# Attention followed by a mixing block on one core: local attention's result turned in 64x64 tiles for two chunks at once, the transposed x kept in staging tiles, and a new order

## The chip, the cores and the metric

The kernel runs on one core of one Trainium2 chip. The core has a matrix engine (TensorE, "PE" in the profile, with its weight loads as "PEld"), a vector engine (VectorE, "DVE"), an activation engine (ScalarE, "ACT"), a general one (GpSimd, "POOL") and one that only issues transfers (SyncE, "SP"). Matmuls write PSUM, eight banks of 512 float32 columns on 128 partitions; all else lies in SBUF. The metric is the time of one execution on the device, in microseconds (us); the figure given for a kernel is the median of its runs.

## The reference

Two parts follow each other. The first is an attention with a coarse and a local branch, for 8 batches, 8 heads, 576 positions and 64 values a head:

```python
q_d = q.reshape(B, H, Sd, factor, D).mean(axis=3)      # factor 4, so 144 positions; k_d, v_d alike
out_d = sm_attn(q_d, k_d, v_d)
out_up = np.repeat(out_d, factor, axis=2)
mask = np.abs(pos[:, None] - pos[None, :]) < factor
scores = scale * np.matmul(q, k.transpose(0, 1, 3, 2))
scores = np.where(mask, scores, -1000000000.0)
...
out_local = np.matmul(attn, v)
return (out_up + out_local).astype(np.float32)
```

Its result, 576 rows of 512 a batch, is the x of the second:

```python
theta = x @ w_theta
zr, zi = x * np.cos(theta), x * np.sin(theta)
y = np.einsum('ts,bsd->btd', w_tok_r, zr) + np.einsum('ts,bsd->btd', w_tok_i, zi)
u = x + y
return (u + np.maximum(u @ w_ch, 0.0)).astype(np.float32)
```

## The kernel before

All matmuls are in bfloat16. The work of a batch is cut into steps, and each step is a small function that issues a few instructions on one engine. `ORDER` is one long list of two-letter words, each with a place behind it (a PSUM bank or two, a staging tile, or the engine that does a copy: v, a or g for DVE, ACT, POOL). The program goes through the list and ties each instruction to the one before it on its engine, so every engine runs its instructions strictly in the order of the list; among engines only data and buffers make them wait. SP issues the loads, the stores and the transposing transfers, in that same order. Nothing else schedules; how the list came about is not in the program.

A batch goes like this. q and k are loaded in float32 into staging tiles (`lq`, `lk`, 14 tiles of 576 columns), cast (`cq`, `ck`), transposed on PE (`tp`, nine 128x128 blocks a step) and copied out of PSUM (`ev`); for the last batch transfers do the turning. Means over four positions (`kd`, `qd`), the coarse scores (`sd`), their exponentials on ACT (`ed`), the coarse result (`nd`), its division (`xn`) and turn (`xd`, `xc`) give xdT, the coarse part with channels on partitions.

The local branch cuts the 576 positions into ten windows of 64 (58 of them own rows), two windows to a chunk, so five chunks. `ps` makes scores for two chunks at once (32 matmuls in 64x64 tiles, L483), `ex` their exponentials, `mk` the multiplication with the band, `po` the product with v of one chunk (16 matmuls in 64x64 tiles, L512), `nm` divides by the row sums (L520 and L521) into tmp. In tmp 64 rows of a window stand twice, heads 0 to 3 on the first 64 partitions and 4 to 7 on the others. `xt` (L524 to L533) turns it: four matmuls of the whole array a chunk, tmp as weights and 116 columns of the identity, into one bank. `xa` (L535 to L541, DVE) adds xdT, each column four times, and writes xT, which is x with channels on partitions.

From xT `th` makes theta (L548, four matmuls of 512 columns for 128 rows), `cs` cosine and sine on ACT. x is also wanted with rows on partitions: `xm` turns it on PE, and for batches 6 and 7 (`XDMA`) `dx` does so with four transposing transfers on SP into one buffer xx (L589). `zz` (L592) multiplies it with cosine and sine. The last 64 rows of a batch take a way of their own (`tt`, `ct`, `zt`, `zp` or `dz`, `zc`). `mx` multiplies with the token weights, nine matmuls of 288 columns a step (L610), `ua` adds x (L615), `ch` is the product with w_ch (L635), `up`/`uc` or `du` turn u back, `rl` (L638, DVE) takes the maximum and adds, `st` stores 128 rows. `ht`, `rt`, `ss`, `sr` do the same for the last 64 rows of two batches at once.

`wm` puts matmuls of zeros into the list where PE would stand still; they compute nothing. 46 of them and six ahead of the list stand in the first 20 us. `te` and `ts` have ACT load the table of exponentials or of sines.

## Time and profile before

| What | Figure |
|---|---|
| Median of three runs | 235.89 us (235.51 to 235.91) |
| The profiled execution | 236.41 us |
| Its span, first to last instruction | 234.7 us |
| PE busy | 223.5 us, 95% of the span |
| DVE, ACT, POOL busy | 187.6, 159.7, 143.9 us |
| Mean granted clock of PE | 0.997 of full speed |
| Transfers | 49.35 MB, 210 GB/s on the mean |

The span lies within the execution; 1.7 us are outside it. In the views of the trace a row of time reads: start in us, length in us, engine, line, operation, tile written and tiles read, shape, number of such instructions in a row, and in brackets how long the engine had been idle and what ended that. A row of groups reads: line, engine, operation, tiles, shape and count, then busy time and the mean of one in ns, then idle time ahead of them. 128\*128 or 64\*64 ahead of a matmul's shape is the part of the array in use, rows by columns. The length of a matmul has its way through the array in it, so two in a row overlap; how long PE is taken by one is the difference between its start and that of the next. "issue" is time in which an engine waited for nothing that the profile shows. A stretch reads: from, to, its length, the busy time and count of PE, PEld, DVE, ACT and POOL, the granted clock, the busy share of the transfer engines, and GB/s.

### The profile page before, as it was taken

To read this page: it belongs to the slowest core of one execution; us is meant where nothing else is said; L and a number is where in the kernel's file an instruction comes from. 1 tells how busy PE (TensorE), PEld (TensorE's weight loads), DVE (VectorE), ACT (ScalarE), POOL (GpSimd) and SP (SyncE) were. 2 spreads that over 40 slices of the span, in tenths; PEclk is the share of its full clock that TensorE was granted. 3 is DMA by queue.
4 is the path that set the end of the run, shared out by engine and by line. 5 is a ranking of instruction groups with operands and counts; after the bars stand their busy time and mean duration, and the time that the engine had idled before them with its cause. 6 is when DMAs were issued, how large, how long until landed. Compare 5 with 4: busy or idle time off the path is not lost.

```text
span 234.7 us, 8524 instructions
## 1 busy us (share of the span) xinstructions
PE 223.5 (95%) x3500; PEld 155.7 (66%) x3500; DVE 187.6 (80%) x377; ACT 159.7 (68%) x239; POOL 143.9 (61%) x190
## 2 busy tenths in 40 slices
PE   7998899999999699999999999899999999999992
PEld 3555767687787466786688757676676665577740
DVE  5169997999898689888799869969898879466472
ACT  2389898669987779869987796859889358510000
POOL 7858999809999995983874628794598310100000
PEclk9999999999999999999999999999999999999998
DMA  6999979996959999999986206996967357674477
GB/s 196 383 392 386 287 163 276 391 244 143 290 162 250 243 345 212 224 224 244 287 183 173 61 0 141 292 236 139 127 155 169 73 124 197 91 221 109 110 226 244
DMA packets 76647, 49.35 MB, mean 210 GB/s; under 512 B 61120, under 2 KB 61120, under 8 KB 76608
## 3 DMA queue, kind: packets, MB, share of 16 engines
q1 hardware_dynamic: 76608, 48.81, 81.4%
q8 instruction: 27, 0.44, 0.8%
q14 instruction: 12, 0.10, 0.2%
HBM read 33.98 MB, written 9.44 MB: 185 GB/s over the span
## 4 chain that ended last, share of the span: by engine, by line
PE 85%; DVE 8%; issue 3%; DMA 2%; ACT 1%; SPq 0%; DVEq 0%
PE PS L610 29%; PE PS L635 12%; PE PS L548 10%; PE PS L304 5%; PE PS L531 3%; PE PS L512 3%; PE PS L715 3%; PE PS L587 2%; PE PS L483 2%; DMA z<-zT 2%; PE PS L275 2%; DVE tmp L521 2%; PE PS L448 2%; PE PS L624 2%; PE PS L652 1%
## 5 line engine op out<-in xcount | busy, mean ns | idle before, releaser
L610 PE MATMUL PS<-WT,z 128*128 128x288 bf16 x576 | 77.9, 286 | 0.4 <-DMA z<-zT 0.4
L610 PEld LDWEIGHTS <-z 128*128 128x128 bf16 x576 | 54.3, 98 | 16.0 <-DMA z<-zT 0.7
L615 DVE TENSOR_TENSOR uT<-PS,xT 128x288 bf16<-128x288 f32 x64 | 28.8, 452 | 12.4 <-PE PS L610 11.9
L548 PE MATMUL PS<-wth,xT 128*128 128x512 bf16 x128 | 32.2, 379 | 0.0
L635 PE MATMUL PS<-wch,uT 128*128 128x512 bf16 x128 | 31.1, 379 | 0.0
L569 POOL TENSOR_TENSOR zT<-xT,cst 128x512 bf16<-128x512 bf16 x7 | 8.1, 1153 | 35.9 <-ACT cst L566 27.6
L521 DVE TENSOR_TENSOR tmp<-PS,rl 128x512 bf16<-128x512 f32 x40 | 27.6, 691 | 1.4
L502 POOL TENSOR_TENSOR pm<-pm,band 128x1024 bf16<-128x1024 bf16 (+1 forms) x14 | 25.1, 1792 | 5.5 <-ACT pm L491 5.5
L537 DVE TENSOR_TENSOR xT<-PS,xdT 128x464 bf16<-128x464 f32 (+1 forms) x40 | 24.0, 628 | 4.5 <-PE PS L531 2.3
L640 DVE SCALAR_TENSOR_TENSOR osb<-PS,ur 128x512 f32<-128x512 f32 x32 | 21.8, 684 | 5.2 <-PE PS L635 4.9
L491 ACT ACTIVATE pm<-PS 128x1024 bf16<-128x1024 f32 (+1 forms) x24 | 20.4, 880 | 6.4 <-PE PS L483 6.4
L553 ACT ACTIVATE cs<-PS,pihc 128x512 bf16<-128x512 f32 x32 | 22.1, 692 | 3.0 <-PE PS L548 2.8
L331 POOL TENSOR_TENSOR two<-kT 128x580 f32<-128x580 bf16 x13 | 15.0, 1154 | 9.4 <-ACT kT L317 6.6
L720 ACT ACT_TABLE_LOAD x15 | 19.2, 1283 | 0.3
L635 PEld LDWEIGHTS <-uT 128*128 128x128 bf16 x128 | 11.9, 98 | 11.1
L554 ACT ACTIVATE cs<-PS 128x512 bf16<-128x512 f32 x32 | 19.2, 600 | 0.0
L594 DVE TENSOR_TENSOR z<-PS,cs 128x1024 bf16<-128x1024 bf16 x24 | 16.0, 681 | 2.4 <-PE PS L587 2.1
L548 PEld LDWEIGHTS <-xT 128*128 128x128 bf16 x128 | 11.2, 98 | 9.8 <-DVE xT L537 0.4
L438 ACT ACTIVATE pd<-PS 128x864 bf16<-128x864 f32 x16 | 13.8, 888 | 5.6 <-PE PS L427 5.6
L331 POOL TENSOR_TENSOR two<-qT 128x576 f32<-128x576 bf16 x13 | 14.9, 1148 | 4.3 <-ACT qT L317 4.0
L397 POOL CAST v_w<-st 128x512 bf16<-128x512 f32 x26 | 16.2, 647 | 0.0
L531 PE MATMUL PS<-ident,tmp 128*128 128x116 bf16 (+1 forms) x160 | 13.9, 215 | 2.1 <-issue 2.0
(116 smaller groups left out, 435.8 us busy)
## 6 DMA issues: line engine op xcount, KB each, us to landing
st<-in_k_dram SPq DMA_DIRECT2D x32, 288.0 KB, 5.3
st<-in_q_dram SPq DMA_DIRECT2D x32, 288.0 KB, 5.9
st<-in_v_dram SPq DMA_DIRECT2D x70, 128.0 KB, 5.0
out_dram<-osb SPq DMA_DIRECT2D x32, 256.0 KB, 3.0
st<-in_v_dram SPq DMA_DIRECT2D x4, 288.0 KB, 3.4
st<-in_moe_w_tok_r_dram SPq DMA_DIRECT2D x4, 288.0 KB, 6.3
st<-in_moe_w_tok_i_dram SPq DMA_DIRECT2D x4, 288.0 KB, 6.1
st<-in_moe_w_theta_dram SPq DMA_DIRECT2D x4, 256.0 KB, 7.2
```

The lines of the kernel that those rows point to most:

```text
L331: nc.gpsimd.tensor_tensor(out=t, in0=src[:, :, 0:2], in1=src[:, :, 2:4], op=ALU.add)
L491: nc.scalar.activation(out=pm[(3 * b + u) % NPM][:, :, 0:n].rearrange("p e c j w -> p e (c j w)"), in_=at.pop(("ps", b, u))[:, :, 0:4 * W ...
L502: EW[w].tensor_tensor(out=t, in0=t, in1=m, op=ALU.mult)
L521: nc.vector.tensor_tensor(out=tmp[(NCH * b + c) % NTMP].rearrange("p g (j d) -> p g j d", d=D), in0=ps[:, :, :, 0:D], in1=r.unsqueeze(3).t ...
L531: nc.tensor.matmul(out=ps[:, kk::2, STEP * g:STEP * g + OWN[n]], lhsT=t[:, g, P * kk:P * kk + P], rhs=identw[:, :, lo:lo + OWN[n]], start= ...
L537: nc.vector.tensor_tensor(out=xT[b % 2][:, :, CH * c:CH * c + cnt].rearrange("p e (m j) -> p e m j", j=4), in0=at.pop(("xt", b, c))[:, :, ...
L548: nc.tensor.matmul(out=ps, lhsT=xT[b % 2][:, dc, P * c:P * c + P], rhs=wth[:, dc, :], start=(dc == 0), stop=(dc == 3))
L553: nc.scalar.activation(out=t[:, 0, :], in_=ps, func=AF.Sin, bias=pihc, scale=1.0)
L610: nc.tensor.matmul(out=ps, lhsT=z[b % 2][:, j, P * dc:P * dc + P], rhs=WT[:, j, cols], start=(j == 0), stop=(j == 8))
L615: nc.vector.tensor_tensor(out=uT[b % 2][:, dc, cols], in0=at.pop(("mx", b, i)), in1=xT[b % 2][:, dc, cols], op=ALU.add)
L635: nc.tensor.matmul(out=ps, lhsT=uT[b % 2][:, dc, P * c:P * c + P], rhs=wch[:, dc, :], start=(dc == 0), stop=(dc == 3))
L640: nc.vector.scalar_tensor_tensor(out=o, in0=at.pop(("ch", b, c)), scalar=0.0, in1=ur[b % 2][:, c, :], op0=ALU.max, op1=ALU.add)
```

## The change

`xt` now handles a unit of two chunks (three units a batch: two chunks, two, one), in a pair of banks. It is cut into 64x64 tiles: a head's 64 channels of one window are the weights, 64x64, and 58 columns of the identity pass through; the two halves of tmp's partitions write different banks, and two heads in a row write different halves of the partitions. A chunk takes 16 such matmuls instead of four. `xa` adds for a unit, so three additions a batch instead of five, up to 928 columns each.

For batches 6 and 7 the transposing transfers write two staging tiles a batch, named in the list, instead of xx; `zz` reads x as two pieces of 256 columns. The staging tiles become 16, in one allocation. The last block of the last batch (batch 7, block 3) is done in two halves of 256 columns: `ch` as eight matmuls, `rl` and `rm` for the two halves, `st` and `su` to store them. A `wm` word can end in one matmul of a smaller width. The whole list is new: 13 groups of warm matmuls (55.4 of 512 columns together) instead of eight, six and seven table words instead of seven and eight, and other engines for some copies.

```diff
-NSTG = 14
+NSTG = 16
 ORDER = """
-l10 l11 c1g c1g k0 l12 lk3 l14 ckg c1v lk5 wm0k t101 c1g e1a kcg wm24 t123 e1a lq6 wm45 x12 cva ckg x13 cva x10 cvv
+l10 c1a l11 c1v wm0g2 t101 l12 l13 c1v c1v lq4 lk5 e1a lk6 k0 cqg kca kca wm255 t123 e1a wm466 x12 x13 kcg lk7 ckg cka
...
-    xx = one([P, 4, DM], "xx") if XDMA else None
...
-    stg = tiles(NSTG, [P, S], "st", FP32)
+    stga = one([P, NSTG, S], "st", FP32)
+    stg = [stga[:, i, :] for i in range(NSTG)]
...
-    def xt(b, c, w):
-        ps = at["xt", b, c] = bank(w).rearrange("p (e t) -> p e t", e=4)
-        t = tmp[(NCH * b + c) % NTMP]
-        for g in range(2):
-            n = 2 * c + g
-            lo = STEP * n - W0[n]
-            for kk in range(2):
-                nc.tensor.matmul(out=ps[:, kk::2, STEP * g:STEP * g + OWN[n]],
-                                 lhsT=t[:, g, P * kk:P * kk + P], rhs=identw[:, :, lo:lo + OWN[n]],
-                                 start=True, stop=True)
+    def xt(b, u, w):
+        ps = at["xt", b, u] = pair(w).rearrange("p k (x n) -> p (k x) n", x=2)
+        for i, c in enumerate(UNITS[u]):
+            t = tmp[(NCH * b + c) % NTMP]
+            for g in range(2):
+                n = 2 * c + g
+                lo = STEP * n - W0[n]
+                for j in range(4):
+                    for hf in range(2):
+                        r = slice(W * hf, W * hf + W)
+                        nc.tensor.matmul(out=ps[W * (j % 2):W * (j % 2) + W, 2 * hf + j // 2,
+                                                CH * i + STEP * g:CH * i + STEP * g + OWN[n]],
+                                         lhsT=t[r, g, D * j:D * j + D], rhs=ident[r, W * hf + lo:W * hf + lo + OWN[n]],
+                                         start=True, stop=True)
...
-    def xa(b, c, w):
-        cnt = OWN[2 * c] + OWN[2 * c + 1]
+    def xa(b, u, w):
+        lo = 2 * CH * u
+        cnt = min(2 * CH, S - lo)
         nc.vector.tensor_tensor(
-            out=xT[b % 2][:, :, CH * c:CH * c + cnt].rearrange("p e (m j) -> p e m j", j=4),
...
+            out=xT[b % 2][:, :, lo:lo + cnt].rearrange("p e (m j) -> p e m j", j=4),
...
-    def dx(b, dc, w):
-        nc.sync.dma_start_transpose(out=xx[:, :, P * dc:P * dc + P], in_=xT[b % 2][:, dc, 0:512])
+    def dx(b, i, w):
+        x = (DXS[b][i // 2] > DXS[b][1 - i // 2])
+        dc = 2 * x + i % 2
+        nc.sync.dma_start_transpose(
+            out=stg16[:, DXS[b][i // 2], 0:2 * DM].rearrange("p (c d) -> p c d", c=4)[:, :, P * (i % 2):P * (i % 2) + P],
+            in_=xT[b % 2][:, dc, 0:512])
...
     def zz(b, c, w):
-        x = xx[:, c, :] if b in XDMA else at.pop(("xm", b, c))
+        if b in XDMA:
+            nc.vector.tensor_tensor(out=z[b % 2][:, 2 * c:2 * c + 2, :].rearrange("p r (k e) -> p r k e", k=2),
+                                    in0=dxr(b, c).unsqueeze(1).to_broadcast([P, 2, 2, 256]),
+                                    in1=cs[(4 * b + c) % NCS].rearrange("p r (k e) -> p r k e", k=2), op=ALU.mult)
+            return
...
+        return [slice(0, DM // 2), slice(DM // 2, DM)] if (b, c) == (B - 1, 3) else [slice(0, DM)]
...
     def rlf(b, c, w):
-        o = at["o", b, c] = osb[(4 * b + c + b // 2) % NOSB]
-        nc.vector.scalar_tensor_tensor(out=o, in0=at.pop(("ch", b, c)), scalar=0.0, in1=ur[b % 2][:, c, :],
-                                       op0=ALU.max, op1=ALU.add)
+        out_part(b, c, halves(b, c)[0])
+
+    def rm(b, c, w):
+        out_part(b, c, halves(b, c)[1])
...
-            for _ in range(int(place[1], 36)):
-                nc.tensor.matmul(out=bank(place[0]), lhsT=warm[:, 0:P], rhs=warm, start=True, stop=True)
+            for n in [512] * int(place[1], 36) + [64 * int(place[2])]:
```

What stands in the engines' rows at three places. First PE, batch 0, where the last chunk's turn (tmp_91) ends between other work of the whole array; before:

```order
L531 MATMUL PS<-ident,tmp_91 128x2x54
L531 LDWEIGHTS tmp_91
L531 MATMUL PS<-ident,tmp_91 128x2x54
L548 LDWEIGHTS xT_101
L548 MATMUL PS<-wth,xT_101 128x512
```

The turn ends with the last of its four matmuls, which has all 128 partitions and two heads' 54 columns, and theta's matmul follows. Now, at the same place:

```order
L533 MATMUL PS<-ident,tmp_91 64x54
L533 LDWEIGHTS tmp_91
L533 MATMUL PS<-ident,tmp_91 64x54
L552 LDWEIGHTS xT_101
L552 MATMUL PS<-wth,xT_101 128x512
```

The last of sixteen matmuls of one head and half the partitions stands there, and theta's matmul, of the whole array, follows in both. Second DVE, batch 0, from the division of chunks 2 and 3 (tmp_89, tmp_90) on, where xT_101 is x turned, kT_63 a copy of k, z_103 a product; before:

```order
L520 RECIPROCAL rl_93<-PS 128x8
L521 TENSOR_TENSOR tmp_89<-PS,rl_93 128x512
L520 RECIPROCAL rl_94<-PS 128x8
L521 TENSOR_TENSOR tmp_90<-PS,rl_94 128x512
L537 TENSOR_TENSOR xT_101<-PS,xdT_99 128x4x116 x4
L520 RECIPROCAL rl_93<-PS 128x8
L521 TENSOR_TENSOR tmp_91<-PS,rl_93 128x512
L317 COPY kT_63<-PS 128x2x576
L537 TENSOR_TENSOR xT_101<-PS,xdT_99 128x4x112
L594 TENSOR_TENSOR z_103<-PS,cs_105 128x1024
```

The products z follow the last addition at once. Now:

```order
L519 RECIPROCAL rl_94<-PS 128x8
L520 TENSOR_TENSOR tmp_90<-PS,rl_94 128x512
L541 TENSOR_TENSOR xT_101<-PS,xdT_99 128x4x232 x2
L519 RECIPROCAL rl_93<-PS 128x8
L520 TENSOR_TENSOR tmp_91<-PS,rl_93 128x512
L316 COPY kT_63<-PS 128x2x576
L541 TENSOR_TENSOR xT_101<-PS,xdT_99 128x4x112
L322 TENSOR_REDUCE kd_67<-kT_63 128x2x5x29
L278 COPY WT<-PS 128x576
L616 TENSOR_TENSOR z_103<-PS,cs_105 128x1024
```

Two additions of 4x232 replace four of 4x116, and a mean over k (kd_67) and a copy of the turned token weights (WT) now stand ahead of the first product. Third DVE, its last instructions, where ur is u turned back and utr that of the last 64 rows; before:

```order
L640 SCALAR_TENSOR_TENSOR osb_120<-PS,ur_115 128x512
L640 SCALAR_TENSOR_TENSOR osb_121<-PS,ur_115 128x512
L640 SCALAR_TENSOR_TENSOR osb_122<-PS,ur_115 128x512
L640 SCALAR_TENSOR_TENSOR osb_123<-PS,ur_115 128x512
L656 SCALAR_TENSOR_TENSOR osb_119<-PS,utr 128x512
```

The four blocks of batch 7 come in a row, and the last 64 rows of batches 6 and 7 end it. Now:

```order
L667 SCALAR_TENSOR_TENSOR osb_120<-PS,ur_114 128x512
L667 SCALAR_TENSOR_TENSOR osb_121<-PS,ur_114 128x512
L667 SCALAR_TENSOR_TENSOR osb_122<-PS,ur_114 128x256
L695 SCALAR_TENSOR_TENSOR osb_118<-PS,utr 128x512
L667 SCALAR_TENSOR_TENSOR osb_122<-PS,ur_114 128x256
```

The last block's second half stands ahead of the last 64 rows, its first half behind them.

117 lines of the change are left out of this document (68 added, 49 removed).

## The prediction, on record before the changed kernel ran

> **What bounds the kernel now.** I read the page first, then the busy time of each engine in stretches of 10 us, then TensorE's instructions in order of time, and last the waits. From the page (engines; chain that ended last; DMA queues):
>
> ```profile
> span 234.7 us, 8524 instructions
> PE 223.5 (95%) x3500; PEld 155.7 (66%) x3500; DVE 187.6 (80%) x377; ACT 159.7 (68%) x239; POOL 143.9 (61%) x190
> ...
> q8 instruction: 27, 0.44, 0.8%
> ...
> PE 85%; DVE 8%; issue 3%; DMA 2%; ACT 1%; SPq 0%; DVEq 0%
> ```
>
> 85% of the last chain is matmuls. The stretches show since when:
>
> ```profile
> 10.00:20.00 10.00, 9.52 (x164) 5.91 (x165) 6.21 (x11) 8.47 (x12) 6.14 (x11) 1.00 1.05 394
> 20.00:30.00 10.00, 8.58 (x234) 6.50 (x223) 9.26 (x19) 8.91 (x12) 10.00 (x14) 1.00 0.96 316
> 30.00:40.00 10.00, 10.00 (x146) 6.98 (x146) 8.73 (x18) 9.16 (x16) 9.61 (x14) 1.00 0.90 206
> ```
>
> PE, the first busy column, is full from 30 us on; ahead of that it waits for loads, casts and softmax, and part of its "busy" is warm matmuls that compute nothing. So the time is: PE's counted work, plus what PE loses in the head, plus its waits later, plus the tail behind its last matmul. I work the change out in these four. Busy figures of single matmuls overlap, so prices are differences of start times, from PE in order of time:
>
> ```profile
> 29.07 0.32 PE L512 MATMUL PS<-v_w,pm 64*64 64x65 bf16 x16
> 29.35 1.04 PE L548 MATMUL PS<-wth,xT 128*128 128x512 bf16 x4
> ...
> 44.59 1.28 PE L610 MATMUL PS<-WT,z 128*128 128x288 bf16 x9
> 45.80 0.77 PE L512 MATMUL PS<-v_w,pm 64*64 64x65 bf16 x32
> ...
> 48.14 0.45 PE L512 MATMUL PS<-v_w,pm 64*64 64x65 bf16 x32
> 48.52 0.47 PE L448 MATMUL PS<-vd,pd 128*72 128x65 bf16 x8
> ...
> 52.62 0.79 PE L531 MATMUL PS<-ident,tmp 128*128 128x116 bf16 x12
> 53.25 1.26 PE L610 MATMUL PS<-WT,z 128*128 128x288 bf16 x9
> 54.35 0.67 PE L304 MATMUL PS<-ident,k_tm 128*128 128x128 bf16 x9
> ...
> 57.01 0.63 PE L560 MATMUL PS<-xT,wth 128*128 128x64 bf16 x16
> 57.47 0.39 PE L587 MATMUL PS<-ident,xT 128*128 128x128 bf16 x4
> ...
> 66.50 0.32 PE L512 MATMUL PS<-v_w,pm 64*64 64x65 bf16 x16
> 66.66 0.54 PE L427 MATMUL PS<-qd,kd 64*64 64x144 bf16 x24
> ```
>
> **The turns on PE (xt).** Now: 12 matmuls of 128x116 take 53.25 - 52.62 = 0.63, so 52.5 ns each; 160 of them (16 a little narrower) take 8.3 us. Then: 640 matmuls in 64x64 tiles, 58 columns each. Nearest row is L512, the same tiles in the same alternation: 16 take 0.16 ahead of other 64x64 work (10 ns each), 32 take 0.38 with the leaving of the mode in it. Leaving costs 0.12 (x16 is 0.28 ahead of L548, 0.16 ahead of L427), entering 0.11 (nine L610 take 1.21 ahead of L512, 1.10 ahead of L304). So 32 cost 0.26, 8 ns each. Bounds: 7.5 ns (8.3 scaled by 58/65) to 10 ns, 4.8 to 6.4 us; I take 8 ns, 5.1, since groups of 32 are what the change has. Saved: 3.2 us.
>
> But each xt that stands between whole-array steps now enters and leaves the mode. Counted in the order of PE's steps, mode changes go from 81 to 111: of the 24 new turns 2 have small-tile neighbours on both sides, 18 on one, 4 on none. 30 changes by 0.10 (0.12 at most) cost 2.9 to 3.6. Net: between -0.6 and +1.5 us; I take **-0.3**. The turns alone gain almost nothing.
>
> **DVE (xa) and the other engines.** The adds, and the products that read the transposed x:
>
> ```profile
> L537 DVE TENSOR_TENSOR xT<-PS,xdT 128x464 bf16<-128x464 f32 x32 | 19.3, 631 | 4.0 <-PE PS L531 1.9 <-ACT xdT L471 1.9
> L594 DVE TENSOR_TENSOR z<-xx,cs 128x1024 bf16<-128x1024 bf16 x8 | 5.3, 682 | 0.1
> ...
> L537 DVE TENSOR_TENSOR xT<-PS,xdT 128x448 bf16<-128x448 f32 x8 | 4.9, 615 | 0.5 <-PE PS L531 0.5
> ```
>
> 16 columns more cost 16 ns, so 1 ns a column: 928 columns take 0.631 + 0.464 = 1.10 us. 16 of these and 8 of 0.615 are 22.5 us against 25.1: 2.6 less on DVE. Yet the new order gives DVE work of POOL's and ACT's (counted step by step at the durations of the groups: two more evictions of k and q, two more means, three more casts of v, four more copies of ur, two more zT); DVE ends with some 5 us more than its 187.6, POOL with 13 less than its 143.9. DVE stays under PE's total, so this is priced at nothing; the cover is PE's full stretch, and where it is gone stands under the rivals. Two exponential/sine pairs fewer take two table loads off ACT, which was 68% busy: nothing.
>
> The transposes of x go to staging tiles, one pair a batch, so batch 7's no longer wait for batch 6's last product. They gain lead before products whose matmuls come some 10 us later, behind mx of batch 6: nothing. SP issues as many as before. Should the products' operand, now two pieces of 256 columns, lose its speed (1 ns a column would be 1.2 us for 0.68), four of them ahead of mx(6,0) add 2 us at worst; I take 0, as width and type of the inner rows stay long.
>
> **The head.** Rows that set it before:
>
> ```profile
> 18.44 1.12 ACT L317 COPY qT<-PS 128x1152 bf16<-128x1152 bf16 x1 [0.24 <-PE PS L304]
> 20.05 1.94 ACT L491 ACTIVATE pm<-PS 128x1024 bf16<-128x1024 f32 x2
> ...
> 22.06 1.67 ACT L438 ACTIVATE pd<-PS 128x864 bf16<-128x864 f32 x2
> ...
> 24.05 0.43 PE L448 MATMUL PS<-vd,pd 128*72 128x65 bf16 x8 [0.73 <-DVE tmp L521]
> ...
> 40.55 1.64 PE L610 MATMUL PS<-WT,z 128*128 128x288 bf16 x12
> ```
>
> I walked the new order through such durations. Warm matmuls come to 55.4 of 512 columns instead of 46. Four of that width, in the list of the last chain:
>
> ```profile
> 55.02 0.86 PE PS L548 x4
> ```
>
> At 0.216 each, that is 2.0 us more that PE can't give back. Last q transposes at 17.3, their copy until 18.95, scores at 19.05 (before: 19.41). Exponentials until 21.4, two of the mean branch until 23.05, so nd at 23.1: it uses banks that po does not hold, and the 0.73 wait goes. th(0,0) at 29.0 (before 29.35), after the first two-chunk add. Then DVE is the chain: second add done at 29.75, after it nm 0.9, kT 1.35, last add 0.6, a mean 1.35, six WT copies 2.7, four products 2.7, zT 0.75, z 0.4: 10.8, so z is whole at 40.5 and mx(0,0) starts at 40.45, 0.1 earlier than before. But PE has done less by then: 21.4 us of counted work instead of 22.8 (two score groups of batch 1 still stand behind it). Lost in the head: 40.45 - 21.4 = 19.05 instead of 40.55 - 22.8 = 17.75: **+1.3**, give or take 1 (a dozen handovers at some 0.1). Behind it stands one more warm group of 0.23: **+0.25**.
>
> **The waits behind the head.** From 40.55 to PE's end 230.2 are 189.65 us; counted work of 185.4 leaves 4.2 us of waits. Three are large:
>
> ```profile
> 75.79 0.46 PE L483 MATMUL PS<-qT,kT 64*64 64x64 bf16 x32
> ...
> 79.29 0.33 PE L531 MATMUL PS<-ident,tmp 128*128 128x116 bf16 x3
> ...
> 81.64 0.23 PE L531 MATMUL PS<-ident,tmp 128*128 128x116 bf16 x1 [2.02 <-issue]
> ...
> 149.07 1.74 DVE L502 TENSOR_TENSOR pm<-pm,band 128x512 bf16<-128x512 bf16 x1
> 151.70 0.32 PE L512 MATMUL PS<-v_w,pm 64*64 64x65 bf16 x16 [0.94 <-DVE tmp L521]
> ...
> 202.16 0.30 PE L610 MATMUL PS<-WT,z 128*128 128x288 bf16 x1 [0.41 <-DMA z<-zT]
> ```
>
> At 79.6 PE stands 2.02 us within a group whose operands are there. 7000 PE instructions over 27 instruction packets are 259 a packet, about 130 matmuls with their loads; from 75.79 to that stop 140 matmuls pass in 3.8 us. I read it as the next packet not there in time: small matmuls use one up faster than it comes, with the DMA engines full. [...] The new order has 998 more PE instructions, but spreads them: cut where the packets were cut, 130 matmuls take 5.1 us or more everywhere behind the head at the prices above, where before single packets held 3.9 and 4.4. So this wait goes: -2.0. At 149 a DVE multiplication lasts 1.74 us beside POOL's and its successor lets PE wait 0.94; the new order has other neighbours there: -1.0, with +1 as likely elsewhere in the bounds. The wait for z (0.41) and the small ones stay. Sum: **-3.0**, bounds -4 and +1.
>
> **The tail.**
>
> ```profile
> 229.39 0.69 DVE L640 SCALAR_TENSOR_TENSOR osb<-PS,ur 128x512 f32<-128x512 f32 x1 [0.17 <-PE PS L635]
> 230.25 0.69 DVE L656 SCALAR_TENSOR_TENSOR osb<-PS,utr 128x512 f32<-128x512 f32 x1 [0.17 <-PE PS L652]
> ...
> 230.97 1.12 SPq L661 DMA_DIRECT2D out_dram<-osb  x2
> ```
>
> Now the last block is added at 229.39, the last 64 rows of two batches at 230.25, and two stores end it. Then the last block comes in halves, but DVE has its second half ahead of the add for those 64 rows and its first half behind it: some 0.4 us more of DVE and a third store on SP (0.55) ahead of the last one: **+0.45**, between 0 and 0.7. The halved matmuls cost PE nothing (eight of 256 for four of 512).
>
> **Sum.** -0.3 + 1.3 + 0.25 - 3.0 + 0.45 = -1.3. The profiled execution took 236.41 us for its span of 234.7, so it would be 235.1; the median, 235.89, lies 0.5 under the profiled one and becomes **234.6 us**.
>
> **Rivals.** (1) *DVE becomes the bound, slower.* For: in program order DVE has 40.2 us of work in PE's counted 150 to 190 us, before 33.8, so a late operation there goes through to PE. Against: from 40 to 80 us both orders have some 40.7 in 40, and before lost only the 2.02 there. Half of DVE's 5 us on the path adds 2.5: 237.1. It decides once waits on DVE behind the head are 1.8 us more than forecast. (2) *The instruction wait stays or moves*, since there are 14% more instructions and DMA is as full: +2.0, 236.6. (3) *Head as good as before and no wait but small ones*: -1.3 and -0.6: 232.8. For it speaks that q, k and the first adds come earlier in my walk; against, DVE's 10.8 us. (4) *Small matmuls cost their full latency.* Sixteen L560 of 64 columns take 0.46, 29 ns each; 640 at that price are 18.5 for 5.1, +13.4: 248. The rows of L512 speak against it. [...]
>
> **Chances.** Under 0.2% (0.47 us) a measurement of this kernel can't be told from no change. Forecast 0.50 (own range 233.6 to 235.8; 0.42 faster, 0.08 same), DVE 0.22 (slower), instruction wait 0.10 (0.08 slower, 0.02 same), better head 0.15 (faster), full latency 0.03 (slower). Faster 0.57, same 0.10, slower 0.33. The range takes in rivals 1 to 3 and the bounds of head and waits: 232.7 to 237.4.
>
> **What would show it.** Right: xt at 8 to 9 ns a matmul with 0.1 steps at its edges; mx(0,0) at about 40.5; no "issue" wait near 2 us on PE; DVE's last half add behind that of the 64 rows. Wrong: PE's idle before 30 us smaller than before with mx(0,0) well under 40; PE waits by DVE between 150 and 190; an issue wait elsewhere.

## The result, and the profile after

The changed kernel took 243.95 us, median of four runs (242.91 to 244.55), beside 235.7 of the kernel before: 1.0362 times as long (95% interval 1.03 to 1.0424). Forecast was 234.6, faster, and 237.4 at most. Run again, unaltered, in a later comparison it took 241.99 (six runs, 241.29 to 244.07), 1.0281 times the kernel before (1.0232 to 1.0329). The change makes the kernel some 3% slower.

The profiled execution took 243.76 us. From its page (span; engines; granted clock in 40 slices; instruction packets; chain that ended last):

```profile
span 242.1 us, 9499 instructions
PE 228.8 (95%) x3999; PEld 155.6 (64%) x3999; DVE 191.6 (79%) x368; ACT 161.1 (67%) x245; POOL 131.2 (54%) x172
...
PEclk9999999999999999999999999999999999799997
...
q8 instruction: 31, 0.51, 1.0%
...
PE 79%; DVE 9%; ACT 6%; issue 4%; DVEq 0%; ACTq 0%
```

The kernel is still bound by PE. What is new is a hole in the granted clock in slice 35 (206 to 212 us), and shares of DVE, ACT and issue in the chain where there was more PE. The stretches, columns as before:

```profile
20.00:30.00 10.00, 8.50 (x316) 6.43 (x314) 9.25 (x19) 9.31 (x13) 9.81 (x13) 1.00 1.09 312
...
50.00:60.00 10.00, 8.64 (x198) 6.46 (x197) 8.25 (x16) 6.05 (x10) 5.99 (x9) 1.00 1.19 209
...
200.00:210.00 10.00, 7.37 (x49) 3.70 (x48) 6.16 (x9) 4.14 (x9) 1.15 (x1) 0.91 0.51 94
```

PE is idle for 1.4 us in 50 to 60 and for 2.6 in 200 to 210, where before it lost nothing and 0.4. Its instructions in order of time, at those places:

```profile
3.79 5.20 PE L755 MATMUL PS<-warm 128*128 128x512 bf16 x17
...
41.64 0.53 PE L632 MATMUL PS<-WT,z 128*128 128x288 bf16 x3
...
58.73 0.60 PE L552 MATMUL PS<-wth,xT 128*128 128x512 bf16 x2 [1.36 <-issue]
...
206.34 0.90 PE L632 MATMUL PS<-WT,z 128*128 128x288 bf16 x6 [2.13 <-DVE osb L667]
207.74 0.54 PE L632 MATMUL PS<-WT,z 128*128 128x288 bf16 x3 [0.50 <-DVE z L611]
208.12 1.76 PE L552 MATMUL PS<-wth,xT 128*128 128x512 bf16 x4
```

Here mx(b,i) is step i of mx for batch b, and likewise for the other steps. mx(0,0) starts at 41.64 instead of 40.55. The instruction wait has moved from 81.64 to 58.73. mx(6,0), at 206.34, waited 2.13 us for an add on DVE, and the four matmuls at 208.12 then take 1.55 (start to start 208.12 to 209.67) instead of 0.86, at the lower clock. The 0.50 is the product at 206.21, which takes 1.47 us beside a multiplication on POOL at 205.98 (0.68 in late_rl and warmcut below, where the two don't meet). DVE there, and SP's queue:

```profile
201.34 1.28 DVE L611 TENSOR_TENSOR z<-st,cs 128x1024 bf16<-128x1024 bf16 x2
205.60 0.69 DVE L667 SCALAR_TENSOR_TENSOR osb<-PS,ur 128x512 f32<-128x512 f32 x1 [2.98 <-issue]
206.21 1.47 DVE L611 TENSOR_TENSOR z<-st,cs 128x1024 bf16<-128x1024 bf16 x1
```

```profile
191.45 1.19 SPq L601 DMA_TRANSPOSE st<-xT  x1
...
193.89 4.93 SPq L601 DMA_TRANSPOSE st<-xT  x3
198.87 1.26 SPq L641 DMA_TRANSPOSE ur<-uT  x1
200.24 1.20 SPq L577 DMA_TRANSPOSE z<-zT  x1
201.54 1.21 SPq L641 DMA_TRANSPOSE ur<-uT  x1
202.84 1.93 SPq L601 DMA_TRANSPOSE st<-xT  x1
```

The add at 205.60 is rl(5,0). It needs ur, whose last quarter, du(5,3), was issued at 201.54 and landed at 205.52. Behind it on DVE stands zz(6,3), the last product for mx(6,0), and bank 3, which rl(5,0) has to release, is the bank mx(6,0) was given. So one transfer holds up PE in two ways. SP is a queue without a gap from 191.45 on, a train of transfers: a transposing transfer takes it some 1.3 us to issue, some 1.9 to 2.3.

A common measure for all that follows: at each mx(b,i), the time lost so far is its start minus PE's counted work ahead of it (start differences where nothing waits: 1.10 for an mx, 0.86 for a th or ch, 0.505 for nine transposes, 0.097 for a mode change, and so on; warm matmuls count as lost). From one profile each:

| Profile | lost in the head, at mx(0,0) | from there to mx(5,4) | from there to PE's end | counted work | behind PE's end |
|---|---|---|---|---|---|
| before | 18.0 | 4.4 | 0.8 | 206.8 | 4.65 |
| after | 20.1 | 5.4 | 4.65 | 206.5 | 5.4 |
| after, again | 18.9 | 6.1 | 4.2 | 206.5 | 5.4 |

After minus before, from the first two rows: head 2.1, middle 1.0, the last stretch 3.9, counted work -0.35, tail 0.7: 7.4 us of span, which is the difference of the two spans (242.1 and 234.7).

### The profile page after: what moved, and what is told of

The parts are those of the page before. It is cut to its first block, busy times and chain, and to the rows that moved or that the text cites. A ratio compares the mean times of both kernels' runs of the same rounds, so it can differ in the third digit from the quotient of the medians.

```text
span 242.1 us, 9499 instructions
## 1 busy us (share of the span) xinstructions
PE 228.8 (95%) x3999; PEld 155.6 (64%) x3999; DVE 191.6 (79%) x368; ACT 161.1 (67%) x245; POOL 131.2 (54%) x172
## 4 chain that ended last, share of the span: by engine, by line
PE 79%; DVE 9%; ACT 6%; issue 4%; DVEq 0%; ACTq 0%
PE PS L632 25%; PE PS L662 11%; PE PS L552 11%; PE PS L303 4%; PE PS L755 4%; PE PS L511 3%; PE PS L482 2%; PE PS L533 2%; PE PS L591 2%; PE PS L274 2%; PE PS L564 2%; PE PS L646 2%; PE PS L691 1%; PE PS L447 1%; PE PS L452 1%
## 5 line engine op out<-in xcount | busy, mean ns | idle before, releaser
L632 PE MATMUL PS<-WT,z 128*128 128x288 bf16 x576 | 79.3, 289 | 2.6 <-DVE osb L667 2.1
L552 PE MATMUL PS<-wth,xT 128*128 128x512 bf16 x128 | 33.3, 386 | 1.6 <-issue 1.4
L501 POOL TENSOR_TENSOR pm<-pm,band 128x1024 bf16<-128x1024 bf16 (+1 forms) x15 | 26.5, 1767 | 10.8 <-ACT pm L490 10.7
L662 PE MATMUL PS<-wch,uT 128*128 128x512 bf16 (+1 forms) x132 | 31.1, 373 | 0.0
L490 ACT ACTIVATE pm<-PS 128x1024 bf16<-128x1024 f32 (+1 forms) x24 | 20.5, 879 | 10.8 <-PE PS L482 10.0
L667 DVE SCALAR_TENSOR_TENSOR osb<-PS,ur 128x512 f32<-128x512 f32 (+1 forms) x33 | 22.0, 670 | 6.6 <-issue 3.0
L541 DVE TENSOR_TENSOR xT<-PS,xdT 128x928 bf16<-128x928 f32 (+1 forms) x24 | 22.4, 950 | 1.8 <-PE PS L533 1.2
L652 POOL COPY ut<-uT 128x256 bf16<-128x256 bf16 x5 | 2.0, 398 | 37.9 <-DVE uT L637 37.9
L437 ACT ACTIVATE pd<-PS 128x864 bf16<-128x864 f32 x16 | 13.9, 890 | 8.8 <-PE PS L426 8.8
L552 PEld LDWEIGHTS <-xT 128*128 128x128 bf16 x128 | 11.1, 98 | 12.8 <-issue 3.2
L330 POOL TENSOR_TENSOR two<-qT 128x576 f32<-128x576 bf16 x11 | 12.8, 1162 | 6.1 <-ACT qT L316 4.5
L296 POOL CAST k_tm<-st 128x576 bf16<-128x576 f32 x22 | 14.6, 672 | 2.1 <-DMA st<-in_k_dram 2.1
L755 PE MATMUL PS<-warm 128*128 128x512 bf16 (+5 forms) x61 | 15.7, 390 | 0.0
```

The lines of the kernel that those rows point to most:

```text
L330: nc.gpsimd.tensor_tensor(out=t, in0=src[:, :, 0:2], in1=src[:, :, 2:4], op=ALU.add)
L490: nc.scalar.activation(out=pm[(3 * b + u) % NPM][:, :, 0:n].rearrange("p e c j w -> p e (c j w)"), in_=at.pop(("ps", b, u))[:, :, 0:4 * W ...
L501: EW[w].tensor_tensor(out=t, in0=t, in1=m, op=ALU.mult)
L541: nc.vector.tensor_tensor(out=xT[b % 2][:, :, lo:lo + cnt].rearrange("p e (m j) -> p e m j", j=4), in0=at.pop(("xt", b, u))[:, :, 0:cnt].r ...
L552: nc.tensor.matmul(out=ps, lhsT=xT[b % 2][:, dc, P * c:P * c + P], rhs=wth[:, dc, :], start=(dc == 0), stop=(dc == 3))
L632: nc.tensor.matmul(out=ps, lhsT=z[b % 2][:, j, P * dc:P * dc + P], rhs=WT[:, j, cols], start=(j == 0), stop=(j == 8))
```

## The experiments

Behind each kernel's median stands how many times as long it took as the kernel before, measured beside it, with the 95% interval.

**The same kernel again.** 

> The changed kernel, unaltered, beside the others on one chip. Theory A (the 4.7 us at 201 to 213 us and the 1.36 at 57 us hang on when single transfers land, which differs from execution to execution): the median lies between 240.5 and 244, and its trace shows the waits at DVE's add of batch 5 and at a border of an instruction block, with other lengths than before, from 0.5 to 3 us each. Theory B (they follow from the order alone): both are there within 0.3 us of their lengths, 2.1 and 1.4, and the median is 243.5 to 244.5.

241.99 us. The waits of PE, and its warm matmuls at the start:

```profile
3.79 4.10 PE L755 MATMUL PS<-warm 128*128 128x512 bf16 x17
...
56.84 0.60 PE L552 MATMUL PS<-wth,xT 128*128 128x512 bf16 x2 [0.66 <-issue]
71.27 0.22 PE L511 MATMUL PS<-v_w,pm 64*64 64x65 bf16 x3 [0.71 <-issue]
...
206.05 2.32 PE L632 MATMUL PS<-WT,z 128*128 128x288 bf16 x9 [2.33 <-DVE osb L667]
```

Both theories got half. The wait for DVE's add is there in both, at the same step (2.13 and 2.33). The instruction wait varies: 1.36 at one border, then 0.66 and 0.71 at two. And the head differs by 1.2 us (20.1 against 18.9 lost) with nothing changed: the 16 warm matmuls of 512 columns and the one of 128 behind them take from 3.79 to 8.83 in one execution and to 7.73 in the other, since the clock goes from half to full speed (0.427 to 0.216 a matmul) at 6.8 us in one and 4.6 in the other.

**The last stretch: DVE's order, SP's queue, the clock.** First the add alone:

```diff
-ch6 rl dt zz dx th4 cs th5 dxe rt tt2 mx3 ua cs cs th4 rl ct mx5
+ch6 dt zz dx th4 cs th5 dxe rt tt2 mx0 ua cs cs th4 rl rl ct mx5
```

> The changed kernel, with the add of batch 5's block 0 moved on DVE from ahead of the last product of batch 6 to just ahead of the add of block 1, and the first mx of batch 6 in bank 0, which is free, instead of bank 3, which that add must release. Theory A (the order on DVE: an add that waits for a transposing transfer holds the product and the bank behind it): mx(6,0) starts at about 204.2 instead of 206.34, the second wait of 0.50 inside it goes too, and the clock has no idle stretch to fall in, so its 2.35 us go as well: 239.0 us, some 5 less than the changed kernel's 243.95. Theory B (SP is full there, every transposing transfer is late and the wait only moves on): the next banks, held until the add for 64 rows and the add of block 1 are done, let PE wait 1 to 2 us at mx(6,2) or mx(6,3): 241 to 242.5. Theory C (the lower clock has nothing to do with the wait): the wait goes, the clock's 2.35 stay: 241.3.

240.31 us, 1.0173 (1.0087 to 1.0259). PE and DVE:

```profile
208.43 1.26 PE L633 MATMUL PS<-WT,z 128*128 128x288 bf16 x9 [1.18 <-DVE osb L696]
...
```

```profile
207.68 0.69 DVE L696 SCALAR_TENSOR_TENSOR osb<-PS,utr 128x512 f32<-128x512 f32 x1 [4.52 <-DMA utr<-ut]
```

mx(6,0) starts at 204.01, as theory A had it, and the clock stays full. But DVE now stands 4.52 us at the add for the 64 rows, whose transfer is the next but one in SP's queue, and mx(6,2) waits 1.18 for the bank that add holds: theory B's place, to the bank. The time lost from mx(5,4) on falls from 4.65 and 4.2 to 1.95. So theory A is right about this add and wrong about the cause behind it. The next link too:

```diff
-th5 dxe rt tt2 mx0 ua cs cs th4 rl rl ct mx5 dx cs ua zz st zz zz mx7 zz
+th5 dxe tt2 mx0 ua cs cs th4 rl rl rt ct mx5 dx cs ua zz st zz zz mx1 zz
```

> As late_rl (the add of batch 5's block 0 behind the last product of batch 6, the first mx of batch 6 in a free bank), and besides the add for 64 rows behind the add of block 1 on DVE, and mx(6,2) in a bank that is free instead of the one that add releases. Theory A (the order on DVE and the banks): no PE wait over 0.3 us is left between 200 and 213 us, PE's time from mx(5,4) to mx(6,4) comes to its counted 24.1 us (28.7 in the changed kernel, 25.9 in late_rl): 1.5 to 2 us less than late_rl in that stretch, 238.5 us. Theory B (SP's transposing transfers are late by themselves): something that reads them still makes PE wait 1 us or more there: 240 or more.

240.96 us, 1.0213 (1.0168 to 1.0257); late_rl and late_full can't be told apart by their times. PE and DVE:

```profile
215.47 1.75 PE L633 MATMUL PS<-WT,z 128*128 128x288 bf16 x13 [1.67 <-DVE osb L668]
```

```profile
211.95 2.50 DVE L612 TENSOR_TENSOR z<-st,cs 128x1024 bf16<-128x1024 bf16 x4 [2.49 <-DMA st<-xT]
```

Between 200 and 213 no wait is left, which theory A asked for; behind it DVE waits 2.49 us for the transposed x of batch 7, with rl(5,2) behind it in its order, and PE 1.67 for the bank of that: theory B. Each time the order is mended, the next reader of SP's queue makes PE wait. So fewer transfers:

```diff
-XDMA = (6, 7)
+XDMA = (7,)
...
-th4 xn dx1 mkv
+th4 xn mkv
...
-xa ztg th6 xa zz ht7 xa cs du th2 dz du dx6 ch3 zz zz ch6 rl dt zz
+xa ztg th6 xa xm0 xm1 zz ht7 zz xa cs du th2 dz du dx6 xm0 ch3 xm1 zz ch6 rl dt zz
```

(The other three words of dx for batch 6 go in the same way.)

> The changed kernel with x of batch 6 turned by PE (16 transposes of 128x128, copied nowhere, read by the products from PSUM, as for batches 0 to 5) instead of four transposing transfers. Theory B (SP's train of transposing transfers, 1.3 us each, one behind the other, is what is late from 191 us on): the transfers for the adds of batch 5 are issued some 5 us earlier relative to the last x of batch 6, the 2.13 + 0.50 + 2.35 us go, PE pays 0.9 for the turns: 239.8 us. Theory A (the order on DVE): the waits go as well, since the add no longer waits, so the two agree on the time; but should the wait stay above 1 us with those transfers landed before it, SP is not its cause: 243 or more.

241.02 us, 1.0203 (1.0141 to 1.0264). PE:

```profile
58.76 0.70 PE L553 MATMUL PS<-wth,xT 128*128 128x512 bf16 x2 [2.14 <-issue]
...
201.95 0.61 PE L592 MATMUL PS<-ident,xT 128*128 128x128 bf16 x8 [0.98 <-DVE xT L542]
...
208.49 1.27 PE L633 MATMUL PS<-WT,z 128*128 128x288 bf16 x9
```

The adds no longer wait, nor does mx(6,0); what PE loses behind mx(5,4) is 1.2, of which 0.98 is its own wait at the new transposes for an addition on DVE, and it works 0.9 more. With the four transfers gone du(5,3) lands at 203.96, 4.5 us ahead of mx(6,0): SP's queue is what PE waited for. (A second part of its lateness is shown under the wait for instructions.) The expected 239.8 was not reached. Its profiled execution, 2.6 us above its median, lost 2.14 us in an instruction wait, and the clock fell behind that too (0.53 granted from 59 to 61 us, 0.61 from 61 to 63).

The clock by itself: ten warm matmuls ahead of mx(6,0), nothing else changed.

```diff
-rt tt2 mx3 ua
+rt tt2 wm0a0 mx3 ua
```

> The changed kernel with ten warm matmuls of 512 columns (2.16 us) ahead of mx(6,0), where PE stood idle for 2.13 and 2.33 us in the two profiles of it. Theory A (the low clock behind that wait, 0.51 to 0.64 for some 4 us, comes of PE's standing still for over 2 us): the granted clock stays at 1.00 in 200 to 212 us though the products come no earlier; the stretch from mx(6,0) to mx(6,4) takes 5.7 to 6.3 us (8.5 and 7.8 in those profiles, 5.3 of counted work): 1.5 to 2.3 less, 240.3 us by the second profile. Theory B (the clock falls there for another reason): the clock is as low and the time is the same or up to 2 us longer: 242 to 244.

Stretches of the changed kernel, then of this one (granted clock behind POOL's count):

```profile
208.00:210.00 2.00, 2.00 (x9) 0.89 (x7) 1.34 (x3) 0.09 (x1) 0.00 (x0) 0.57 0.51 74
210.00:212.00 2.00, 2.00 (x11) 1.31 (x10) 0.00 (x0) 1.09 (x2) 0.00 (x0) 0.58 0.77 226
```

```profile
206.00:208.00 2.00, 1.78 (x12) 0.90 (x10) 1.87 (x4) 0.00 (x0) 0.17 (x1) 1.00 0.41 83
208.00:210.00 2.00, 2.00 (x18) 1.59 (x17) 0.96 (x2) 1.18 (x2) 0.00 (x0) 1.00 0.75 121
```

The products come no earlier (mx(6,0) 20.5 us behind mx(5,4), against 20.2 and 20.45), the clock stays full, and mx(6,0) to mx(6,4) takes 6.53 us instead of 8.49 and 7.79. Theory A holds, at 1.3 to 2.0 us rather than 1.5 to 2.3; the 2.35 of earlier expectations had the wait of 0.50 in it, and the 5.3 of counted work should be the 6.13 that late_full and late_pe take there. The median, 241.22 (ratio 1.0265, 1.0223 to 1.0307), is only 0.8 below the unaltered kernel's and not separable from it by its interval.

The staging of x for batch 7:

```diff
-dz du dx6 ch3
+dz du dx1 ch3
...
-th5 dxe rt
+th5 dx5 rt
```

> The changed kernel with the two staging tiles of batch 7's x made the same as batch 6's, so that batch 7's transposing transfers wait for batch 6's last product, as with the one buffer of the kernel before. Theory A (the transfers stand in SP's order, so a waiting one holds all behind it): the first transfer of batch 7 starts when the last product of batch 6 has read its tiles, at about 207.7 instead of 202.84; the transfer for the 64 rows behind it comes 5 us later, the add on DVE that needs it holds mx(6,2)'s bank, and the time grows by 3 to 5 us: 245 to 249. By the prediction, which priced the staging at nothing: within 0.5 of the changed kernel.

245.61 us, 1.045 (1.0384 to 1.0516), but it does not test what it should: in this order batch 7's first transfer stands ahead of three products of batch 6, so it overwrote the x that they then read, and they waited for it (PE's wait at mx(6,0) grew to 3.61). It shows that the new order needs the separate tiles; what they are worth by themselves stays open.

**The wait for instructions.** The stops lie at PE instruction 193 + 256n of the program, to the instruction: 2753 (n = 10) before, 1985 (n = 7) after. An instruction packet is a transfer of 16 KB on a queue of its own (q8 in the page: 27 packets and 0.44 MB before, 31 and 0.51 MB after), and in every profile there is one for each such border; while loads run it starts between 0.8 us ahead of PE's passing the border before and 4.5 us after it in the 16 profiles. In the kernel before the border was passed at 75.88, the packet ended at 80.16 and PE went on at 81.64; in the changed one 52.44, 57.14, 58.73. First the border is moved, in the kernel before:

```diff
-            for _ in range(int(place[1], 36)):
-                nc.tensor.matmul(out=bank(place[0]), lhsT=warm[:, 0:P], rhs=warm, start=True, stop=True)
+            width = 128 if place[1] == "k" else 512
+            for _ in range(int(place[1], 36) * 512 // width):
+                nc.tensor.matmul(out=bank(place[0])[:, 0:width], lhsT=warm[:, 0:P], rhs=warm[:, 0:width],
+                                 start=True, stop=True)
```

> The kernel before, with its first group of warm matmuls as 80 of 128 columns instead of 20 of 512: the same columns, 120 more instructions on PE ahead of all else, so every later border between blocks of 256 PE instructions falls 120 instructions earlier in the program. Theory A (the 2.02 us at 79.6 are the wait for the next block of instructions, since its 256 passed in 3.8 us): the block is now cut across a slower stretch and the wait goes: 233.7 to 234.3. Theory B (the block is late for transfers in that stretch whatever the border): the wait stays, at an instruction 120 earlier: 235.7. Theory C (it has nothing to do with instructions): it stays at the same matmul of the program, 235.7.

No instruction wait over 0.2 us is left behind 28 us, so theory A has the cause. Yet the time is 237.51, 1.009 (1.005 to 1.013): 0.9% slower. PE and DVE:

```profile
194.93 0.37 PE L531 MATMUL PS<-ident,tmp 128*128 128x116 bf16 x4 [1.57 <-DVE osb L640]
```

```profile
194.18 0.69 DVE L640 SCALAR_TENSOR_TENSOR osb<-PS,ur 128x512 f32<-128x512 f32 x1 [1.82 <-DMA out_dram<-osb]
```

PE comes to mx(5,4) 1.0 us earlier (180.49 for 181.47), and loses it again at 195 us, where an add waits for a store to leave its output buffer; stores stand in SP's queue as well. That store was issued at 189.96 and landed 4.20 us later, beside an instruction packet (191.04 to 192.68), where in the kernel before the one issued at 191.19 landed after 2.38: the shift of the borders has put a packet there. With a sixth buffer and all warm matmuls halved:

```diff
-    NOSB = 5
+    NOSB = 6
...
-    warm = one([P, 512], "warm")
+    warm = one([P, 256], "warm")
...
-            for _ in range(int(place[1], 36)):
-                nc.tensor.matmul(out=bank(place[0]), lhsT=warm[:, 0:P], rhs=warm, start=True, stop=True)
+            for n in range(2 * int(place[1], 36)):
+                nc.tensor.matmul(out=bank(place[0])[:, 0:256], lhsT=warm[:, 0:P], rhs=warm, start=True, stop=True)
```

> The kernel before, with every warm matmul cut into two of 256 columns (104 more instructions on PE ahead of the wait at 79.6 us, the same columns) and six output buffers instead of five. In before_shift the instruction wait went and 1.57 us came back at 195 us, where an add on DVE waited 1.82 us for a store to leave its output buffer. Theory A (stores stand behind transposing transfers on SP, one more buffer is enough): neither wait is there: 233.5 to 234.5, faster than both kernels. Theory B (SP's train of transposing transfers sets the time there): the wait comes back at the adds or products that read them: 235.5 to 237.5.

236.03 us, 1.0025 (0.9984 to 1.0065): no difference from the kernel before. The buffer did its part, nothing is lost from mx(6,0) on; but the instruction wait is back, at the same instruction 2753 and so at another place of the program, and shorter ones besides:

```profile
80.79 0.79 PE L610 MATMUL PS<-WT,z 128*128 128x288 bf16 x5 [1.25 <-issue]
```

The same shift in the changed kernel:

```diff
-            for n in [512] * int(place[1], 36) + [64 * int(place[2])]:
+            wide = [128] * 4 if place == "0g2" else [512]
+            for n in wide * int(place[1], 36) + [64 * int(place[2])]:
```

> The changed kernel with its first group of warm matmuls as 64 of 128 columns instead of 16 of 512: 96 more instructions on PE ahead of all else, so every later border between blocks of 256 falls 96 earlier. Theory A (in the stretch of loads up to 90 us the next block takes up to 6.3 us from its request, and the blocks of this order last 4.8 to 6.3, so any border can be late): PE still waits for instructions at one to three borders, none of them at the matmul of the program where it did at 57 us, 0.5 to 2.5 us together: within 1 us of the unaltered kernel, 241 to 243. Theory B (one dense stretch is to blame, as in the kernel before): no such wait over 0.3 us is left: 240.5.

242.47 us, 1.0295 (1.0249 to 1.0341), the same as unaltered. Its instruction wait now lies in the head, and a low clock behind it:

```profile
26.19 0.33 PE L447 MATMUL PS<-vd,pd 128*72 128x65 bf16 x3 [2.11 <-issue]
```

```profile
26.00:28.00 2.00, 1.81 (x23) 1.81 (x23) 0.90 (x3) 0.00 (x0) 2.00 (x4) 0.50 1.04 377
```

Theory A: waits for instructions now stand at 26, 57, 71 and 81 us in one profile or another. Why they are late, with loads taken away:

```diff
         lo = W0[2 * c + g]
+        if b in (1, 2):
+            return
         nc.sync.dma_start(out=at["v", b, c][W * g:W * g + W].rearrange("p (h d) -> p h d", d=D),
```

> The changed kernel without the loads of v of batches 1 and 2 (20 transfers, 2.6 MB, between 38 and 95 us); these two batches are worked out with what the staging tiles held before, all other work stays. Theory A (the next block of PE instructions is late because its packet stands behind loads that are on their way, which themselves take 6 to 7 us from issue to landing there): with fewer of them the packets requested between 40 and 95 us end 1.0 to 3.5 us after the request instead of 1.7 to 4.7, and no instruction wait over 0.3 us is left behind 40 us; 1 to 1.5 us less than the unaltered kernel, 240.7. Theory B (PE's instruction fetch is as slow whatever the loads do): a wait of 0.5 to 2 us stays at 57 us; 242.

The block of 256 instructions that was late at 57 us runs through: its border is passed at 52.22, the packet ends at 53.78 (57.14 with all loads), and PE goes from step to step:

```profile
55.18 1.04 PE L554 MATMUL PS<-wth,xT 128*128 128x512 bf16 x4
56.05 0.67 PE L303 MATMUL PS<-ident,q_tm 128*128 128x128 bf16 x9
56.55 1.03 PE L554 MATMUL PS<-wth,xT 128*128 128x512 bf16 x4
...
204.99 0.90 PE L634 MATMUL PS<-WT,z 128*128 128x288 bf16 x6 [2.39 <-DVE osb L669]
```

From 40 to 70 us the packets end 0.6 to 2.3 us behind the border, and no instruction wait over 0.2 us is left from 40 us on: theory A. The time is 242.17 (1.0291, 1.0256 to 1.0326), no less than the unaltered kernel's; the wait at mx(6,0) is 2.39 and the clock behind it falls to 0.50 again, and 0.59 of instruction wait stands at 31 us, ahead of the loads taken away.

The packets reach further than PE. The trace shows the landing of a transposing transfer as sixteen parts. In the changed kernel fifteen parts of du(5,3) have landed by 204.01 and the last at 205.52, and a packet is on its way from 203.44 to 204.34. It is so in the other profiles too: of the 266 transposing transfers between 180 and 216 us in the 16 profiles, the 120 with no instruction packet on its way land 2.4 to 2.8 us after their issue starts; of 42 that took over 3.5 us, 41 had a packet for PE beside them, and so had all 31 whose issue took SP over 1.6 us. In after_shift, and in turn_whole and warmcut below, the steps around mx(6,0) stand in the same order but the borders lie elsewhere, and the packet falls on another transfer. There du(5,3) landed 2.42 us after its issue instead of 3.98, the clock stayed at 1.00 from 198 to 210 us, and mx(6,0) waited not at all, 0.77 and 0.23 us. In the order after_shift, warmcut, turn_whole:

```profile
208.71 1.26 PE L632 MATMUL PS<-WT,z 128*128 128x288 bf16 x9
```

```profile
203.46 1.26 PE L633 MATMUL PS<-WT,z 128*128 128x288 bf16 x9 [0.77 <-DVE osb L668]
```

```profile
203.32 1.26 PE L630 MATMUL PS<-WT,z 128*128 128x288 bf16 x9 [0.23 <-DVE osb L665]
```

From mx(5,4) to mx(6,4) PE takes 25.0, 26.2 and 24.9 us in these three, 28.7 and 28.2 in the two profiles of the unaltered kernel. So the large wait at mx(6,0), and the low clock behind it, stand where two things meet: a lead of SP's train that leaves nothing over (12.8 to 13.6 us in these three, not counting waits), and a packet that holds back one part of du(5,3) by 1.5 us.

**The turn by itself.**

```diff
-                for j in range(4):
-                    for hf in range(2):
-                        r = slice(W * hf, W * hf + W)
-                        nc.tensor.matmul(out=ps[W * (j % 2):W * (j % 2) + W, 2 * hf + j // 2,
-                                                CH * i + STEP * g:CH * i + STEP * g + OWN[n]],
-                                         lhsT=t[r, g, D * j:D * j + D], rhs=ident[r, W * hf + lo:W * hf + lo + OWN[n]],
-                                         start=True, stop=True)
+                for kk in range(2):
+                    nc.tensor.matmul(out=ps[:, 2 * kk:2 * kk + 2, CH * i + STEP * g:CH * i + STEP * g + OWN[n]],
+                                     lhsT=t[:, g, P * kk:P * kk + P], rhs=identw[:, :, lo:lo + OWN[n]],
+                                     start=True, stop=True)
```

(The bank of a pair holds other heads then; the addition reads them in the order it needs.)

> The changed kernel, order and additions for two chunks kept, with the turns by the whole array again: four matmuls of 116 columns a chunk into the pair of banks, 160 instead of 640. By the prediction's term the small tiles save 3.2 us and pay 2.9 to 3.6 in mode changes: without them the time is 0.3 longer, 244.2, between 243.3 and 244.6. Rival: the changes of mode or the small turns cost more than counted, and part of the 8 us that the change lost is theirs: 241 to 243. Either way PE has some 960 instructions fewer, so the instruction wait of 1.36 us at 57 us stands elsewhere or goes, which can take another 1.4 off.

240.43 us, 1.0179 (1.0098 to 1.026): some 1% below the unaltered kernel, with overlapping intervals. Groups of the turns, of the changed kernel and of this one:

```profile
L533 PE MATMUL PS<-ident,tmp 64*64 64x58 bf16 x576 | 8.2, 193 | 0.0
```

```profile
L532 PE MATMUL PS<-ident,tmp 128*128 128x116 bf16 x144 | 10.7, 215 | 0.0
```

Start to start it is 8.3 ns for a small turn and 53.0 for a large one. Mode changes fall from 111 to 97 only: the new order has 16 more of them than the old one even with whole turns. So PE's counted work is 208.3 against 206.5: in this order the small tiles save 1.8 us of PE, and not 0.3. They are not where the time went. What turn_whole gains it gains in waits: it has 0.33 us of instruction waits behind 40 us (960 PE instructions fewer), its clock rose at 3.8 us, and its du(5,3) landed 12.4 us behind the first transfer of SP's train instead of 14.1. None of these three is the turn's own price, but the first and the third follow from its number of instructions, which sets where the packets fall.

**The head.**

```diff
-l10 c1a l11 c1v wm0g2 t101
+l10 c1a l11 c1v wm0c2 t101
...
-wm255 t123 e1a wm466 x12
+wm235 t123 e1a wm436 x12
```

> The changed kernel with 9 warm matmuls of 512 columns fewer in the first three groups (12 + 3 + 4 instead of 16 + 5 + 6, the narrow last ones kept). Theory A (PE's order with its warm matmuls is what sets the head): the first turns of v begin when their last cast is done, at about 8.1 instead of 8.83, the ones after it as much earlier, and mx(0,0) starts 0.7 to 0.9 earlier than 41.64: 243.1. Theory B (the head waits for loads and casts): idle time stands where the warm matmuls stood, mx(0,0) stays within 0.2 of 41.64: 243.9. Theory C (the clock needs them): matmuls stay at 0.43 us longer than until 6.8 us and the head gets longer: 244.5 or more.

240.53 us, 1.0212 (1.0132 to 1.0293). PE:

```profile
11.55 1.31 PE L390 MATMUL PS<-ident,xT 128*64 128x128 bf16 x40 [1.05 <-ACT xT L381]
```

mx(0,0) starts at 40.45, 1.2 earlier than in the first profile and level with the second, in an execution whose clock rose late (6.3 us). x12 waits 1.05 for ACT's copy, so the first groups of warm matmuls do stand in the way, as theory A has it, and ACT is next behind them. How much it is worth can't be read from the median, since the rise of the clock alone moves the head by 1.2, and 18 instructions fewer on PE move the packets as well: the one that fell on du(5,3) falls on the transfer for the 64 rows, and mx(6,2) waits 1.02 for the add behind that.

**All together.** late_pe with two more of PE's steps (ht7 and th2) ahead of its first transposes, warmcut, and the tail's add:

```diff
-rm st su rt ss rl st sr
+rm st su rl rt ss st sr
```

> The changed kernel with four edits: x of batch 6 turned by PE and not by transfers (in banks that are free earlier than in late_pe), the 9 warm matmuls of the first three groups left out, the last half add of the last block ahead of the add for the last 64 rows. Theory A (the loss is made of these places): head 0.9 us shorter, the waits and the low clock of 200 to 213 us gone for 0.9 of PE's work, the tail behind PE's last matmul 4.7 instead of 5.4: 5 to 6 us less than the unaltered kernel, 236 to 237.5, with the waits for instructions left. Theory B (what is taken away in one place comes back in the next): 239 or more.

238.69 us, 1.0151 (1.0112 to 1.019), the fastest of the changed kernels, 3.3 below the unaltered one and 3 above the kernel before; its profiled execution was the fastest of six, 237.3. Theory A by the stretches (lost: head 17.9, middle 4.2, behind mx(5,4) 0.7, with 0.9 more work), but the median is 1.2 above its range. The tail stayed at 5.4. SP there, and with the store moved as well:

```profile
231.13 0.49 SPq L701 DMA_DIRECT2D out_dram<-osb  x1
231.68 0.58 SPq L672 DMA_DIRECT2D out_dram<-osb  x1
232.31 0.47 SPq L701 DMA_DIRECT2D out_dram<-osb  x1
```

```diff
-rm st su rl rt ss st sr
+rm st su rl rt st ss sr
```

> As combined, with the store of the last block's first half also ahead of the stores of the last 64 rows on SP. In combined the add was moved and the tail behind PE's last matmul stayed 5.4 us, since that store still stood between the two others. Theory A (SP's third store is the tail's 0.7 us): the tail is 4.7 to 4.8 us, the median 0.6 under that of combined, 238.1. Theory B (landing sets it): 5.3 or more, 238.7.

```profile
230.14 2.25 SPq L672 DMA_DIRECT2D out_dram<-osb  x4
232.48 1.12 SPq L701 DMA_DIRECT2D out_dram<-osb  x2
```

The store is out from between the two others, and the tail is 5.0: half of the 0.7 goes, between the theories. 239.16 us, 1.018 (1.0136 to 1.0223): not to be told from combined. No version here beats the kernel before.

## Why the prediction was wrong, step by step

**Turns and mode changes (-0.3): right.** The small turn takes 8.3 ns (8 forecast), counted work fell by 0.35. turn_whole splits it: the tiles give 1.8, the order's further mode changes take 1.5. Rival 4 (full latency, 248) fell. Two sums in the prediction are a little off: the net's upper bound comes to +1.7 (8.3 - 6.4 saved, 3.6 paid), and rival 3 to 232.7.

**DVE and the adds (nothing): right.** 928 columns took 1.117 us (1.10), DVE 191.6 (some 192.6), POOL 131.2 (13 less). Rival 1 did not come: from 150 to 190 us no wait of PE for DVE reaches 0.3 in the two profiles of the changed kernel.

**The head (+1.3): right in mechanism, within what one execution varies.** By the measure above it grew by 2.1 and by 0.9 us in the two profiles; in nine whose order is the same up to mx(0,0) it is 18.45 to 21.85. What it left out is that the clock's rise, ahead of which a warm matmul takes 0.427 us and not 0.216, came at 3.8 us in one profile (turn_whole) and at 6.8 in another (after), with 0 to 7 slow matmuls behind the first six, and that an instruction wait can fall into the head as well (2.11 us at 26 us in after_shift).

**The waits (-3.0): wrong, with two causes.** The first is "so this wait goes: -2.0". The reading of the wait was right (before_shift, fewer_loads), the price of a packet was not. I took 5.1 us for a block as enough, since single packets had come in 3.9 and 4.4, and as the least that a block would last; the one that ends at 57 us passes in 4.56 us where it runs through (warm_late, late_full). At PE's stop the packet had ended 4.3 us behind the border in the kernel before and 4.7 in the changed one, and a packet ends up to 5.8 behind it in the other profiles while loads are on their way; PE went on 1.5 and 1.6 us after its end: 6 to 7 us, and most of the new order's blocks between 40 and 90 us last 5 to 6.5. Of seven profiles with the same instructions on PE up to 190 us six lost 0.85 to 2.5 us so (late_rl and late_full at 27 and 33 us already), and one (warm_late) nothing over 0.2. That is rival 2, given a tenth. And before_shift shows that even where the wait goes the time may not. The other -1.0, the wait at 149 us, did go; but four of 0.48 (79.26), 0.17 and 0.23 (112) and 0.26 us (171.42) stand elsewhere, 1.1 together. What is left of the growth between mx(0,0) and mx(5,4) lies in differences too small to name.

**The second: the transposes of x by transfers, priced at "nothing. SP issues as many as before."** The number was right, the place was not looked at. Before, the first transposing transfer of batch 6 was issued at 183.62, 17.0 us ahead of mx(6,0); after, at 191.45, and without its wait mx(6,0) would have come at 204.2, 12.8 us behind. Nine transfers are issued from there to du(5,3), and that one landed 14.1 us behind the first issue, 1.5 of them for an instruction packet beside it. Before, the same transfer landed 13.3 us behind the first issue, in a lead of 17.0. SP was not bound on the whole, yet was the bound of this stretch: 2.13 and 0.50 us of wait, then 1.85 at the lower clock (mx(6,0) to mx(6,4) takes 8.49, and 6.13 where nothing waits, as in turn_whole), where the forecast kept 0.41. late_rl, late_full and late_pe show the chain link by link, warm_late the clock's share, and the three profiles with other borders that without the packet on du(5,3) 0 to 0.8 us of the wait is left. The prediction counted issues and not their lead, and it had no term for what an instruction packet does to a transfer. How much of the median hangs on the packet is not shown.

**The tail (+0.45): right in kind.** 0.7 measured, half of it the third store (combined2); the other half stays open.

The misses in the first profile: counted work 0; head 0.8 (2.1 for 1.3); waits 7.7 (1.0 + 3.9 for -3.0 + 0.25); tail 0.25. Together they are the 8.7 us between -1.3 and 7.4.

## What to carry to other kernels

Price a queue of transfers by its lead: the time from its first issue to the first engine that waits for its last landing, against the sum of its issue times, at the place where it is fullest, with some 1.5 us over for an instruction packet that can fall on it (what du(5,3) lost to one here). A change in the number of PE's instructions, even in the head, moved all later packets here (120 more in before_shift, 96 more in after_shift, 18 fewer in warmcut). Look what stands behind each reader of a late transfer on its engine, and which PSUM bank it holds; moving the reader only shows the next. A wait whose length depends on what else is on its way (instruction packets, none to 2.14 us here at one place of the order; a low clock, 1.3 to 2.0) should be carried as a range in every version and not be removed from one.
